# Scan resets, PSUM bank order and two moved steps in the attention units of an RWKV and two-MLP kernel

## The chip, the cores and the metric

The kernel runs on one core of one Trainium2 chip. The metric is the device time of one execution in microseconds; the time of a kernel is the median of several executions. PE is TensorE (matrix products and transposes), DVE is VectorE, ACT is ScalarE, POOL is GpSimd, and SP issues most of the DMAs.

## What is computed

Three stages follow each other: a linear attention with a decaying state (4 batches, 8 heads, 768 positions, head size 48), an expert layer in which each of the 3072 tokens goes to one of 8 experts, and a dense layer with a squared ReLU. In float32, from the reference:

```python
for t in range(S):
    kt, vt, rt, wt = (k[:, :, t], v[:, :, t], r[:, :, t], w[:, :, t])
    cur = np.einsum('bhd,bhe->bhde', u[None] * kt, vt)
    y[:, :, t] = np.einsum('bhd,bhde->bhe', rt, state + cur)
    state = wt[:, :, :, None] * state + np.einsum('bhd,bhe->bhde', kt, vt)
...
logits = x @ w_gate;  e_idx = np.argmax(logits, axis=1)
out[mask] = gate_w[mask, None] * eom[mask, e, None] * (np.maximum(x[mask] @ w1[e], 0.0) @ w2[e])
...
h = x @ w_in;  r = np.maximum(h, 0.0);  return (r * r) @ w_out
```

## The kernel before

**Units.** The attention is cut into 16 units (`NU`), each one batch and two heads, so four units make a batch. A unit's 768 positions are six chunks of 128 (`NC`), each in two halves of 64 (`HT`). For each half, running products of the decay w are needed forwards from the half's start (`ff`, in `prefix`) and backwards from its end (`suf`, in `suffix`). One scan instruction on DVE makes these products for all six chunks at once: the six stretches of 64 lie in a row of 390 with a zero ahead of each stretch, and at that place the scan adds a start value out of the vector `f_1`, so that the running product begins anew there. `suffix` runs two scans: the one of the second half (q = 1) starts from ones (`s_1`); the one of the first half (q = 0) starts from the results of the former, which L688 copies into `f_1`. `prefix` runs two: the first starts from reciprocals (L697), the second from the results of the first, which L699 copies into `f_1`. Both kinds of reset write the same 128x391 vector in turn.

**One iteration of the loop (L843 to L885).** The order of the work on PE, DVE, ACT, SP and POOL is written out by hand: each engine takes its instructions in the order of the calls. Iteration t does, in this order, for the units t - 1, t, t + 1 and t + 2: the loads; `gate_products` of t + 1 (POOL, two products into the one buffer `g1`); `scores` of the first three chunks of t (PE, copied by ACT, masked on POOL by a select, L743); `k_back` of t (PE transposes, copied by ACT into `kP`); `prefix` of t + 1 (DVE); `within` of t - 1 (PE); `states` of t (PE); `state_scan` of t (DVE, L755); `scores` of the last three chunks; `spread` of t + 1 (ACT); `across` of t - 1 (PE, copied by ACT); `k_turn` and `r_turn` of t + 1 (PE transposes, multiplied on DVE by `suf` into `kT`, L708, and by `ff` into `rA`, L713); `w_turn` of t + 2 (PE); `bonus_in` of t (PE, needs the gate values `gv`); `gate_sum` (DVE, L723) and `gate_values` (POOL, L726) of t + 1; `suffix` of t + 2 (DVE); `back` of t - 1 (PE). At t = 0 `gate_sum` and `gate_values` of unit 0 itself come after `prefix` of unit 1.

**Routing.** As soon as a batch has its output, its tokens are routed in small steps that are dealt out over the next units by place and iteration (`PLAN`, `LAST`, places "back", "scan", "turned", "gate"): products with the gate weights on PE, some twenty small operations on DVE, and six indirect scatters into `x_rows` on POOL. For the last batch but one this ends in iteration 15 at the place "scan". `rows_A` (L256, on DVE) works out which token rows the first expert block, block A, gathers; it stands in iteration 15 at the place "back", ahead of `state_scan` of unit 15. In the same iteration eight splits of weights of block A follow on DVE ("turned", L341), the gathers of the rows on POOL ("gate", L402) and, in iteration 16, their scaling on DVE (L413). `finish_routing` sorts the experts by count; L289 there compares with a table `ek` of expert numbers that one iota of POOL makes at the start (L132).

**PSUM banks.** The class `Ring` (L643) hands out four banks in turn to whoever asks: two to the first scores, two to `k_back`, one to `states`, two to the last scores, two each to `k_turn`, `r_turn` and `back`, and one now and then to routing. So which earlier user a step has to wait for depends on the order of the asking. In `k_turn` of t + 1 the first bank is one of `k_back`, the second is that of `states`, which is free when `state_scan` has read it.

**After the units** come block A, one block with few rows, the expert blocks 1 to 7 and the dense layer, all bound together by data: the routing of the last batch is queued on PE behind the transposes of block A's rows.

Of the kernel before, what the change touches and what calls it, by code (L numbers as in the profile page):

```python
# [9 lines left out]
F32 = mybir.dt.float32  # L10
# [4 lines left out]
ALU = mybir.AluOpType  # L15
AX = mybir.AxisListType
# [5 lines left out]
def rwkv_moe_kernel(  # L22
# [15 lines left out]
    nc = tc.nc  # L38
    B, H, S, D = r.shape
    NT, DM = out.shape  # L40
    E, _, F = w1.shape
# [77 lines left out]
    def routing_constants():  # L119
        nonlocal e8, ei, ek, keyc, slot, tile0, over  # L120
        nc.gpsimd.memset(ones, 1.0)
# [9 lines left out]
        ei = iota("ei", [128, E], [[1, E]])  # L131
        ek = iota("ek", [128, E, E], [[1, E], [0, E]])  # L132
        keyc = cst.tile([128, E], F32, name="keyc")
# [12 lines left out]

    e8 = ei = ek = keyc = slot = tile0 = over = None

# [132 lines left out]
    def finish_routing():  # L281
# [6 lines left out]
        nc.vector.tensor_reduce(key, be, axis=AX.X, op=ALU.add)  # L288
        nc.vector.tensor_tensor(be, row(key), ek, op=ALU.is_equal)  # L289
        yield  # L290
# [287 lines left out]
    with ExitStack() as actx:  # L578
# [11 lines left out]
        u_bc = ac.tile([128, H, D], F32, name="u_bc")  # L590
        f_1 = ac.tile([128, NL + 1], F32, name="f1")
        s_1 = ac.tile([128, NL + 1], F32, name="s1")
# [4 lines left out]
        warm = bia[0:1, 2:3]  # L597
        none = f_1[:, 1:L]
        zw = [ps_u.tile([128, NL + 1], F32, name="zw") for _ in range(2)]
# [53 lines left out]
        class Unit:  # L653
# [29 lines left out]
            def suffix(self, z=zw):  # L683

                self.suf = wk.tile([128, 2, NL + 1], F32, name="suf")
                for q in (1, 0):
                    if q == 0:
                        nc.vector.tensor_copy(f_1[:, L::L], self.suf[:, 1, 1::L])  # L688
                    nc.vector.tensor_tensor_scan(out=self.suf[:, q, ::-1], data0=z[q][:, ::-1], data1=(s_1 if q else f_1)[:, ::-1],  # L689
                                                 initial=0.0, op0=ALU.mult, op1=ALU.add)  # L690

            def prefix(self, z=zw):

                self.ff = wk.tile([128, 2, NL], F32, name="ff")
                for q in range(2):
                    if q == 0:
                        nc.vector.reciprocal(f_1[:, 0:NL:L], self.suf[:, 0, 1::L])  # L697
                    else:
                        nc.vector.tensor_copy(f_1[:, 0:NL:L], self.ff[:, 0, HT::L])  # L699
                    nc.vector.tensor_tensor_scan(out=self.ff[:, q], data0=z[q][:, :NL], data1=f_1[:, :NL], initial=0.0, op0=ALU.mult, op1=ALU.add)  # L700

# [27 lines left out]
            def k_back(self):  # L729
                self.kP = wk.tile([128, NC, 2, 64], F32, name="kP", bufs=1)  # L730
                for q, pt in enumerate(self.turn(self.kT)):
                    nc.scalar.copy(self.kP[:, :, q], pt)

            def scores(self, hf):
                A = self.A[hf] = wk.tile([128, HC, 2, C], F32, name=f"A{hf}")
                pa = [ring.tile([128, HC, C], F32, name="pt") for j in range(2)]
                for ci in range(HC):
# [53 lines left out]
        def at(i, st, *a):  # L791
            if 0 <= i < NU:
                getattr(units[i], st)(*a)
# [21 lines left out]
        def first_block_step(t, place):  # L815
# [6 lines left out]
            if NU - 2 <= t < NU and place == "back":  # L822
                for f in range(2 * (t - NU + 2), 2 * (t - NU + 2) + 2):
                    first["A"].prep_w(f, nc.vector, part="hi")
            if (t, place) == (NU - 1, "back"):
                rows_A(rw)
# [16 lines left out]
        for t in range(-1, NU + 1):  # L843
# [6 lines left out]
            first_block_step(t, "loads")  # L850
            if t + 1 < NU - 1:
                at(t + 1, "gate_products")
# [6 lines left out]
            if t == 0:  # L859
                at(t, "gate_sum")  # L860
                at(t, "gate_values")
            at(t - 1, "within")
            at(t, "states")
            at(t, "state_scan")
            at(t, "scores", 1)
            at(t + 1, "spread")
            at(t - 1, "across")
            step(t, "scan")
            at(t + 1, "k_turn")
            at(t + 1, "r_turn")  # L870
# [525 lines left out]
```

## Time and profile before

| | |
|---|---|
| time, median of 3 runs | 844.82 us (844.03 to 846.26) |
| profiled execution, its own time | 843.21 us |
| its span, first to last instruction | 841.4 us, 15700 instructions, mean granted clock 0.991 |
| busy in the span | PE 801.0 us (95%), DVE 543.2 (65%), ACT 374.1 (44%), POOL 351.9 (42%) |
| chain that ended last, by engine | PE 62%, DVE 15%, issue 14%, POOL 4%, DMA 2% |
| costliest lines of DVE in that chain | L689 3%, L700 2%, L713 2%, L708 1%, L755 1% |

The page also cuts the span into 40 slices of 21 us. Each digit is the busy share in tenths (9 is 90% or more):

```profile
PE   5999999878999999999999999999999999999995
DVE  7799999956567777887633878888633434434342
ACT  4566665632544545455544344343433333333321
POOL 7665868535335445544653334243311212223121
PEclk9999999989999999999999999999999999999998
DMA  9576777414659577678751233232204113032011
```

The attention units fill the first eight slices. A share of busy time is an average over what runs in a slice; which engine ends a wait there is read from the timelines. The ends of PE's products are modelled, so PE at 90% is not PE at its peak.

### The profile page before, as it was taken

To read this page: it belongs to the slowest core of one execution; us is meant where nothing else is said; L and a number is where in the kernel's file an instruction comes from. 1 tells how busy PE (TensorE), PEld (TensorE's weight loads), DVE (VectorE), ACT (ScalarE), POOL (GpSimd) and SP (SyncE) were. 2 spreads that over 40 slices of the span, in tenths; PEclk is the share of its full clock that TensorE was granted. 3 is DMA by queue.
4 is the path that set the end of the run, shared out by engine and by line. 5 is a ranking of instruction groups with operands and counts; after the bars stand their busy time and mean duration, and the time that the engine had idled before them with its cause. 6 is when DMAs were issued, how large, how long until landed. Compare 5 with 4: busy or idle time off the path is not lost.

```text
span 841.4 us, 15700 instructions
## 1 busy us (share of the span) xinstructions
PE 801.0 (95%) x5964; PEld 725.0 (86%) x5964; DVE 543.2 (65%) x977; ACT 374.1 (44%) x792; POOL 351.9 (42%) x433
## 2 busy tenths in 40 slices
PE   5999999878999999999999999999999999999995
PEld 4888787758889999999999998888899999999994
DVE  7799999956567777887633878888633434434342
ACT  4566665632544545455544344343433333333321
POOL 7665868535335445544653334243311212223121
PEclk9999999989999999999999999999999999999998
DMA  9576777414659577678751233232204113032011
GB/s 180 117 144 118 159 149 187 164 53 156 207 105 258 137 252 191 188 195 277 142 180 48 93 114 94 76 102 85 76 1 141 45 69 112 11 104 76 1 47 38
DMA packets 157365, 102.90 MB, mean 122 GB/s; under 512 B 112350, under 2 KB 140942, under 8 KB 157286
## 3 DMA queue, kind: packets, MB, share of 16 engines
q1 hardware_dynamic: 149046, 86.55, 38.8%
q0 software_dynamic: 4912, 14.65, 5.3%
q8 instruction: 48, 0.79, 0.4%
q10 hardware_dynamic: 3328, 0.66, 0.4%
q14 instruction: 31, 0.25, 0.1%
HBM read 79.34 MB, written 22.50 MB: 121 GB/s over the span
## 4 chain that ended last, share of the span: by engine, by line
PE 62%; DVE 15%; issue 14%; POOL 4%; DMA 2%; ACT 0%; POOLq 0%; DVEq 0%; SPq 0%; ACTq 0%
PE ph L346 9%; PE ph L347 9%; PE ph L348 9%; PE po L346 5%; PE po L348 5%; PE px L348 5%; PE po L347 5%; PE px L346 5%; PE px L347 5%; DVE suf L689 3%; POOL out_dram L1185 2%; DVE ff L700 2%; DVE rA L713 2%; DVE kT L708 1%; DVE St L755 1%
## 5 line engine op out<-in xcount | busy, mean ns | idle before, releaser
L1160 DVE SCALAR_TENSOR_TENSOR gg<-ph,rl 128x512 f32<-128x512 f32 x96 | 66.2, 689 | 121.8 <-ACT rl L1158 111.3
L1158 ACT ACTIVATE rl<-ph 128x512 f32<-128x512 f32 x96 | 57.4, 598 | 145.8 <-PE ph L348 137.0
L341 DVE TENSOR_TENSOR gl<-gg,gh 128x512 fp32r<-128x512 f32 x96 | 66.7, 695 | 65.9 <-ACT gh L339 41.9
L339 ACT CAST gh<-gg 128x512 fp32r<-128x512 f32 x96 | 59.6, 621 | 103.5 <-DVE gg L1160 103.5
L341 POOL TENSOR_TENSOR w1l<-w1r,w1h 128x384 fp32r<-128x384 f32 x56 | 59.5, 1069 | 66.9 <-ACT w1h L339 66.5
L335 ACT ACTIVATE hh<-ph 128x320 fp32r<-128x320 f32 (+7 forms) x64 | 32.4, 507 | 112.1 <-PE ph L348 99.1
L1106 POOL TENSOR_TENSOR caf<-caf,cbf 128x384 f32<-128x384 f32 x32 | 32.5, 1017 | 114.0 <-DVE cbf L1105 114.0
L341 DVE TENSOR_TENSOR w2l<-w2r,w2h 128x384 fp32r<-128x384 f32 x64 | 63.6, 997 | 20.1 <-ACT w2h L339 19.0
L336 DVE SCALAR_TENSOR_TENSOR hl<-ph,hh 128x320 fp32r<-128x320 f32 (+7 forms) x64 | 36.8, 576 | 36.5 <-ACT hh L335 30.8
L1185 POOL DMA_INDIRECT out_dram<-ob,tokc x24 | 23.4, 975 | 67.2 <-DVE ob L1183 65.0
L346 PE MATMUL po<-hh,w2h 128*128 128x320 f32 (+4 forms) x120 | 42.3, 352 | 0.0
L347 PE MATMUL po<-hl,w2h 128*128 128x320 f32 (+4 forms) x120 | 41.3, 345 | 0.0
L348 PE MATMUL po<-hh,w2l 128*128 128x320 f32 (+4 forms) x120 | 41.2, 344 | 0.0
L341 POOL TENSOR_TENSOR x22l<-x2r,x22h 128x512 fp32r<-128x512 f32 x12 | 15.5, 1293 | 51.5 <-ACT x22h L339 51.5
L740 PE MATMUL pt<-rA,kT 64*128 64x128 f32 x300 | 31.7, 301 | 4.4 <-DVE rA L713 4.4
L341 POOL TENSOR_TENSOR x21l<-x2r,x21h 128x512 fp32r<-128x512 f32 x12 | 15.6, 1296 | 45.5 <-ACT x21h L339 45.5
L402 POOL DMA_INDIRECT xg<-x_rows,gi x28 | 29.0, 1034 | 11.0 <-issue 4.9
L339 ACT CAST w2h<-w2r 128x384 fp32r<-128x384 f32 x64 | 32.9, 516 | 0.0
L247 POOL DMA_INDIRECT x_rows<-xr,dsi x24 | 24.3, 1011 | 20.7 <-DVE vals L240 14.3
L339 ACT CAST w1h<-w1r 128x384 fp32r<-128x384 f32 x64 | 32.7, 512 | 0.0
L743 POOL TENSOR_SCALAR_AFFINE_SELECT A<-A 128x768 f32<-128x768 f32 x32 | 27.7, 873 | 10.4 <-ACT A L742 10.4
L726 POOL TENSOR_TENSOR gv<-vN,g 128x576 f32<-128x576 f32 x16 | 18.4, 1153 | 32.1 <-issue 14.2
(863 smaller groups left out, 2655.1 us busy)
## 6 DMA issues: line engine op xcount, KB each, us to landing
w1r<-in_moe_w_dram SPq DMA_DIRECT2D x16, 768.0 KB
w2r<-in_moe_w_dram SPq DMA_DIRECT2D x16, 768.0 KB
x2r<-x_cols SPq DMA_DIRECT2D x12, 768.0 KB
cq<-in_moe_w_in_dram SPq DMA_DIRECT2D x16, 384.0 KB
cq<-in_moe_w_out_dram SPq DMA_DIRECT2D x16, 384.0 KB
vN<-in_v_dram SPq DMA_DIRECT2D x32, 144.0 KB
part<-ob SPq DMA_DIRECT2D x24, 192.0 KB
ob<-part SPq DMA_DIRECT2D x24, 192.0 KB
```

The lines of the kernel that those rows point to most:

```text
L335: nc.scalar.activation(hi, src, AF.Relu)
L336: nc.vector.scalar_tensor_tensor(lo, src, 0.0, hi.bitcast(F32), op0=ALU.max, op1=ALU.subtract)
L339: nc.scalar.copy(hi, src)
L341: lo_eng.tensor_tensor(lo, src, hi.bitcast(F32), op=ALU.subtract)
L346: nc.tensor.matmul(out_, a_of(ah), b_of(bh), start=start, stop=False)
L347: nc.tensor.matmul(out_, a_of(ah), b_of(bl), start=False, stop=False)
L348: nc.tensor.matmul(out_, a_of(al), b_of(bh), start=False, stop=stop)
L740: nc.tensor.matmul(pa[j][:, ci], self.kT[pp, hf * HC + ci], self.rA[pp, hf * HC + ci], start=True, stop=True)
L1106: nc.gpsimd.tensor_tensor(af, af, bf, op=ALU.add)
L1158: nc.scalar.activation(rl, ph, AF.Relu)
L1160: nc.vector.scalar_tensor_tensor(gg, ph, 0.0, rl, op0=ALU.max, op1=ALU.mult)
L1185: ins = nc.gpsimd.indirect_dma_start(out=out[:, :], out_offset=IndirectOffsetOnAxis(ap=tokc[:, n:n + 1], axis=0), in_=ob, in_offset=None)
```

## The change

- `f_1` gets a second row. The first keeps the resets of the suffix scan and of the first prefix scan, the second holds those of the second prefix scan.
- In `suffix` the copy of the six reset values becomes a reduce with a maximum over one element each.
- In `prefix` one reciprocal of 12 elements, from both halves of `suf`, takes the place of a reciprocal of 6 and a copy of 6. Both scans of `prefix` now start from values that are known before either of them.
- `score_banks` asks for the two banks of the last scores right after `within`, ahead of `states`; the scores themselves stay where they were.
- `rows_A` moves from "back" to a new place "scan" of iteration 15, behind `state_scan`, the last scores, `across` and the last scatter step.
- `gate_products` of unit 1 moves from the start of iteration 0 to behind `gate_values` of unit 0.
- The table `ek` is gone; the comparison reads the vector `ei`, broadcast.

```diff
-        ek = iota("ek", [128, E, E], [[1, E], [0, E]])
...
-        nc.vector.tensor_tensor(be, row(key), ek, op=ALU.is_equal)
+        nc.vector.tensor_tensor(be, row(key), col(ei), op=ALU.is_equal)
...
-        f_1 = ac.tile([128, NL + 1], F32, name="f1")
+        f_1 = ac.tile([128, 2, NL + 1], F32, name="f1")
...
                 for q in (1, 0):
                     if q == 0:
-                        nc.vector.tensor_copy(f_1[:, L::L], self.suf[:, 1, 1::L])
-                    nc.vector.tensor_tensor_scan(out=self.suf[:, q, ::-1], data0=z[q][:, ::-1], data1=(s_1 if q else f_1)[:, ::-1],
+                        nc.vector.tensor_reduce(f_1[:, 0, L::L], self.suf[:, 1, 1::L].rearrange("p (c o) -> p c o", o=1), axis=AX.X, op=ALU.max)
+                    nc.vector.tensor_tensor_scan(out=self.suf[:, q, ::-1], data0=z[q][:, ::-1], data1=(s_1 if q else f_1[:, 0])[:, ::-1],
                                                  initial=0.0, op0=ALU.mult, op1=ALU.add)
...
+                nc.vector.reciprocal(f_1[:, :, 0:NL:L], self.suf[:, :, 1::L])
                 for q in range(2):
-                    if q == 0:
-                        nc.vector.reciprocal(f_1[:, 0:NL:L], self.suf[:, 0, 1::L])
-                    else:
-                        nc.vector.tensor_copy(f_1[:, 0:NL:L], self.ff[:, 0, HT::L])
-                    nc.vector.tensor_tensor_scan(out=self.ff[:, q], data0=z[q][:, :NL], data1=f_1[:, :NL], initial=0.0, op0=ALU.mult, op1=ALU.add)
+                    nc.vector.tensor_tensor_scan(out=self.ff[:, q], data0=z[q][:, :NL], data1=f_1[:, q, :NL], initial=0.0, op0=ALU.mult, op1=ALU.add)
...
+            def score_banks(self):
+                self.pa = [ring.tile([128, HC, C], F32, name="pt") for j in range(2)]
+                return self.pa
+
             def scores(self, hf):
...
-                pa = [ring.tile([128, HC, C], F32, name="pt") for j in range(2)]
+                pa = self.pa if hf else self.score_banks()
...
-            if (t, place) == (NU - 1, "back"):
+            if (t, place) == (NU - 1, "scan"):
                 rows_A(rw)
...
-            if t + 1 < NU - 1:
+            if t and t + 1 < NU - 1:
                 at(t + 1, "gate_products")
...
             if t == 0:
                 at(t, "gate_sum")
                 at(t, "gate_values")
+                at(t + 1, "gate_products")
             at(t - 1, "within")
+            at(t, "score_banks")
             at(t, "states")
...
             step(t, "scan")
+            first_block_step(t, "scan")
```

## Rows read from the trace of the kernel before

**Rows 1.** Busy by stretches: us, PE, PEld, DVE, ACT, POOL, granted clock, DMA share, GB/s:

```profile
84.00:105.00 21.00, 19.49 (x347) 16.65 (x345) 19.80 (x35) 12.81 (x31) 17.46 (x23) 1.00 0.72 160
...
294.00:841.00 547.00, 537.01 (x2758) 493.35 (x2756) 309.56 (x485) 218.93 (x425) 185.56 (x193) 1.00 0.35 106
```

**Rows 2.** Groups by line, 0 to 260 us (count, busy us, mean ns, idle before):

```profile
L688 DVE COPY f<-suf 128x6 f32<-128x6 f32 x16 | 10.9, 680 | 0.6
...
L699 DVE COPY f<-ff 128x6 f32<-128x6 f32 x16 | 6.8, 423 | 0.5
```

**Rows 3.** DVE timeline, one unit: start, us, operation, [idle before <- releaser]:

```profile
34.35 0.41 DVE L688 COPY f<-suf 128x6 f32<-128x6 f32 x1
...
36.02 0.97 DVE L700 TENSOR_TENSOR_SCAN ff<-zw,f 128x390 f32<-128x390 f32 x1
...
37.67 0.97 DVE L700 TENSOR_TENSOR_SCAN ff<-zw,f 128x390 f32<-128x390 f32 x1
38.56 0.73 DVE L755 TENSOR_TENSOR_SCAN St<-pt,P 128x288 f32<-128x288 f32 x1
39.91 0.56 DVE L708 TENSOR_TENSOR kT<-pa,suf 128x384 f32<-128x384 f32 x1 [0.62 <-PE pa L668]
...
43.43 0.41 DVE L688 COPY f<-suf 128x6 f32<-128x6 f32 x1
```

**Rows 4.** DVE timeline, two small operations at 100 to 108 us:

```profile
100.90 2.40 DVE L688 COPY f<-suf 128x6 f32<-128x6 f32 x1
...
107.31 0.22 DVE L186 TENSOR_REDUCE mx<-lg 128x6 f32<-128x48 f32 x1
```

**Rows 5.** POOL timeline, what ran beside those two:

```profile
101.84 1.42 POOL L718 TENSOR_TENSOR g<-kN,rN 128x576 f32<-128x576 f32 x1
...
107.25 0.86 POOL L743 TENSOR_SCALAR_AFFINE_SELECT A<-A 128x768 f32<-128x768 f32 x1 [0.38 <-ACT A L742]
```

**Rows 6.** PE timeline, where a step begins in one unit:

```profile
90.44 0.94 PE L740 MATMUL pt<-rA,kT 64*128 64x128 f32 x12 [0.35 <-DVE rA L713]
...
96.05 0.27 PE L668 MATMUL pt<-ident,kN 64*128 64x64 f32 x1
...
118.02 0.62 PE L668 MATMUL pt<-ident,kN 64*128 64x64 f32 x12
...
120.11 0.86 PE L668 MATMUL pt<-ident,xT 64*128 64x64 f32 x12
```

**Rows 7.** DVE timeline, the first kT product of units 5 and 6:

```profile
58.08 1.02 DVE L708 TENSOR_TENSOR kT<-pt,suf 128x384 f32<-128x384 f32 x2 [0.62 <-PE pt L668]
...
69.08 1.00 DVE L708 TENSOR_TENSOR kT<-pt,suf 128x384 f32<-128x384 f32 x2
```

**Rows 8.** DVE timeline, the first kT product of units 9 and 10:

```profile
97.38 1.02 DVE L708 TENSOR_TENSOR kT<-pt,suf 128x384 f32<-128x384 f32 x2 [0.62 <-PE pt L668]
...
109.56 0.53 DVE L708 TENSOR_TENSOR kT<-pa,suf 128x384 f32<-128x384 f32 x1
```

**Rows 9.** POOL timeline, the first gate product of unit 1:

```profile
17.31 1.42 POOL L718 TENSOR_TENSOR g<-kN,rN 128x576 f32<-128x576 f32 x1 [4.21 <-DVE g L723]
```

**Rows 10.** PE timeline, before and at the bonus of unit 0:

```profile
19.42 0.95 PE L676 MATMUL zw<-ident,wN 64*128 64x64 f32 x12
22.24 0.87 PE L764 MATMUL py<-ident,gv 128*128 128x128 f32 x6 [1.87 <-POOL gv L726]
```

**Rows 11.** Busy time by stretches, 24 to 28 us (columns as in rows 1):

```profile
24.00:26.00 2.00, 2.00 (x27) 1.88 (x25) 1.86 (x5) 1.88 (x5) 1.92 (x3) 0.50 1.13 224
26.00:28.00 2.00, 2.00 (x38) 1.95 (x37) 0.54 (x1) 1.28 (x3) 1.81 (x2) 0.71 0.59 120
```

**Rows 12.** DVE timeline, the end of the units:

```profile
165.62 0.14 DVE L257 TENSOR_SCALAR mA<-cum 128x1 f32<-128x1 f32 x1
...
169.28 0.76 DVE L755 TENSOR_TENSOR_SCAN St<-pt,P 128x288 f32<-128x288 f32 x1 [0.55 <-PE py L781]
...
178.84 0.53 DVE L413 TENSOR_SCALAR xg<-xg 128x384 f32<-128x384 f32 x1 [4.10 <-DMA xg<-x_rows,gA]
```

More of the change, by code (lines that the diff above doesn't have):

```diff
@@ L119, in routing_constants @@
     def routing_constants():
-        nonlocal e8, ei, ek, keyc, slot, tile0, over
+        nonlocal e8, ei, keyc, slot, tile0, over
         nc.gpsimd.memset(ones, 1.0)
@@ L145, in routing_constants @@
         reset_routing()
-    e8 = ei = ek = keyc = slot = tile0 = over = None
+    e8 = ei = keyc = slot = tile0 = over = None
     def reset_routing():
@@ L597, in rwkv_moe_kernel @@
         warm = bia[0:1, 2:3]
-        none = f_1[:, 1:L]
+        none = f_1[:, 0, 1:L]
         zw = [ps_u.tile([128, NL + 1], F32, name="zw") for _ in range(2)]
```

## The prediction

> **What bounds the kernel now.** I read the 40 slices of the page first: PE is nearly full from the second slice to the last, DVE is busy for most of the first fifth of the span and at a third of it later. The table of busy time by stretches says the same in numbers [rows 1]: from 294 us on PE works 537.01 of 547 us at a granted clock of 1.00, so nothing but PE sets the pace there; from 84 to 105 us, inside the attention units, DVE works 19.80 of 21 us and PE 19.49. The change touches only the units (0 to some 170 us). What it takes from them should therefore come off the end one for one, since every later stage starts from data of the one before. The chain of waits, read in order of time, runs through DVE in most units: scan, reset copy, scan, reciprocal, scan, reset copy, scan, state scan, then a short wait for PE, then the products. So the second view is DVE's timeline of one unit without routing [rows 3]: the same copy comes at 34.35 and 43.43, one unit is 9.08 us. The third question is how far behind DVE the next engine is, and that is PE [rows 6].
>
> **Reset copies.** The two groups take 10.9 and 6.8 us for 16 copies each of 128x6 [rows 2], in the mean 680 and 423 ns. One such copy lasts 2.40 us, from 100.90 to 103.30 [rows 4]; beside it POOL runs a product from 101.84 to 103.26 [rows 5], and the copy ends as that ends: it is held by POOL's work. The reduce at 107.31 takes 0.22 us [rows 4] although POOL's select runs from 107.25 to 108.11 [rows 5]. A maximum over one element is such a reduce, with 6 inputs in place of 48, so I price it at 0.19, between 0 and 0.22. The first copy thus gives back 10.9 - 16 x 0.19 = 7.9 us of DVE. The second copy goes altogether, and with it the dependence between the two prefix scans: from one to the next it is 1.65 us now (36.02 to 37.67), while a scan with no dependence behind it lets the next operation start after 0.89 (37.67 to 38.56) [rows 3]. That is 0.76 us in a clean unit. The merged reciprocal writes 12 elements for 6; no row shows that size beside this one, so its growth is bounded by 0 and by one more small operation, 0.22 [rows 4]; I take 0.04, since the reduce over 48 elements needs no more than 0.22 in all.
>
> The Trainium skill (VectorE: DVE Perf Modes, Rules for kernel authors) speaks against this part: a reduce on the hot path is called the slowest operation of this engine, to be expected at single rate. At six elements the row of 0.22 us with 48 inputs does not bear that out as a cost; by the page the rate would matter only for long rows.
>
> **Score and state banks.** Four PSUM banks are handed out in turn. Before, the states' bank came ahead of the two score banks, so the second bank of the next unit's k transposes was the states' bank and had to wait for the state scan: DVE then sits 0.62 us before kT, released by PE [rows 3, 7, 8]. After, that bank is one that ScalarE has copied out long before the state scan, and the states' bank goes to the last r transposes, which DVE needs 0.9 us (two kT products [rows 8]) later. I cost the new order at nothing otherwise; what hides it is across, which PE runs in between. If ScalarE were late, the wait would return, 0.62 at most.
>
> **Clean unit.** DVE: 9.08 - 0.22 (copy to reduce, 0.41 to 0.19) - 0.76 - 0.62 + 0.04 = 7.5 us [rows 3]. PE: from the scores to the next k transposes 5.61 (90.44 to 96.05), from there over r and w transposes and the bonus to the back transposes 2.09 (118.02 to 120.11), the twelve back transposes between 0.4 and the 0.62 of the same twelve [rows 6]: 8.1 to 8.3, and between 0 and 0.35 waiting for rA [rows 6]. I take 8.27. So PE becomes the bound, the unit goes from 9.08 to 8.27, and 0.81 of the 1.56 that DVE gives up reaches the end. Three units run so (2 to 4): 2.4 us. Ends: 0.4 (9.08 - 8.3 - 0.35) and 1.56 each, 1.2 to 4.7.
>
> **Routed units.** Ten units (5 to 14) also carry routing on PE and DVE. In three of them PE has 24 routing products more. One takes 11.00 us with no long copy (58.08 to 69.08 [rows 7]), and there PE, not DVE, is the last to arrive at the state scan: no gain. The other two take 12.2 each (one of them 97.38 to 109.56 [rows 8]) because of the 2.40 us copy; they fall to 11.00, 1.18 each. The remaining seven I put at the clean unit's 0.81: 5.7. Sum 8.0. Ends: the two long copies alone, 2.4, and the full 1.1 of DVE work per unit, 11.
>
> **First gate products.** At the first step POOL starts unit 1's gate product only at 17.31, held 4.21 us for DVE's sum of unit 0 [rows 9], and A's select and unit 0's gate values queue behind its two halves. PE is done with the w transposes at 20.37 and stands until 22.24 for those values [rows 10]. After, the values of unit 0 go first and the products second, and the bonus can start when PE gets there: 22.24 - 20.37 = 1.9 us, and 0.3 for the copies of unit 0, which lie on the same path (an estimate, under the 0.76 of a clean unit): 2.2. Behind the moved products stands the select of unit 0's second scores. Counted from 17.31 it is done at the latest after values no longer than a product, two products and itself: 17.31 + 1.42 + 2.84 + 0.86 = 22.4 [rows 5, 9]; PE wants it after the bonus and the scores, 20.07 + 0.87 + 0.94 = 21.9 at the earliest [rows 6, 10]. So up to 0.5 may be lost to this wait. After PE stood still the granted clock is 0.50, the 1.2 GHz level, from 24 to 26 us, and 0.71 from 26 to 28 [rows 11]; at half pace that costs 1.0 + 0.6 = 1.6 us. If the shorter stand leaves the clock up, this comes back too. Ends 1.7 and 3.8; I take 3.0. The Trainium skill (TensorE: Matmul & The Clock Gate, Part 1) says an idle PE falls to the lower clock; the row agrees, and by that rule the sum would use 3.8.
>
> **First rows.** Their index work runs from 165.62 to 168.73 ahead of the state scan of unit 15, which then waits another 0.55 for PE [rows 12]. Moved behind it, the state scan can only come earlier, but across of unit 15 is not what the gathers wait for; they wait for scatters in POOL's queue. So gain 0. Queued behind the moved work are eight splits of weights, which shift by up to 3.1 us; DVE now stands 4.10 us before 178.84 [rows 12], so 1.0 of cover is left. Without that cover the gathered rows would be scaled late by what exceeds it. One index table less on POOL at the start lies beside the first loads: 0.
>
> **Sum.** 3.0 + 2.4 + 8.0 = 13.4 us against the profiled execution, 843.2 - 13.4 = 829.8; its span is 841.4 and some 1.8 lie around it. The median of the runs shown is 1.6 above that execution, so the forecast against the median 844.8 is 831.4; I say 832, for small waits that pass to ScalarE.
>
> **Rivals.** (1) PE holds the units harder than I summed: every unit costs PE its 8.3 and the whole 0.35 for rA, and in routed units ScalarE's copies add as much again. Then only the start (2.2), the two long copies (2.4) and 0.4 in each clean unit remain, 5.8 us: 839. For it: PE is at 19.49 of 21 now [rows 1]. Against: part of that busy time is PE waiting for the banks. (2) DVE's whole saving comes out, because PE's busy time is partly stretched waiting: the upper ends, 3.8 + 4.7 + 11 = 19.5: 825. Against: the 8.1 of PE are starts in sequence without idle. (3) The reduce is held by POOL as the copy was: then the two long stalls stay, 11 us are left, 834, still within the forecast. (4) Nothing measurable: the units end earlier but the gathers at the end wait for something else. Against: scatters and gathers follow the last unit's gate sums through one queue. 844. (5) Slower, by the clock: tighter units could make PE alternate work and short stands so that the granted clock stays at 0.50 as at 24 us [rows 11]. Each us at half clock loses half a us, so with 13 gained it decides beyond 26 us of such stretches in the units; 32 of them give 844.8 - 13.4 + 16 = 847. Against: PE gets busier, and in the units it stood at 1.00 [rows 1].
>
> **How the numbers follow.** Forecast (827 to 836) 0.72; rival 1 (836 to 842) 0.14; rival 2 below 827 0.05; rival 4 0.06; rival 5 0.03. Rival 3 is inside the forecast. The range 827 to 839 leaves out rival 2's part, the upper part of rival 1 (0.05), 4 and 5: 0.19. 0.3% is 2.5 us, about what a measurement of this kernel can tell from no change: faster 0.91, same 0.06, slower 0.03.
>
> **What would show it.** In the trace after: the reduce at 0.15 to 0.22 us in all 16 units with none near 2; prefix scans 0.9 apart; no wait of DVE before kT released by PE right after the state scan, but one of PE's own making, in clean units of 8.2 to 8.4 us; the bonus of unit 0 near 20 us; the scaling of the first rows still released by the DMA and not by splits. The prediction is wrong if clean units stay near 9 us, if PE's sequence has gaps of its own, or if the end of the units moves and the first products of the experts do not.

## The result and the profile after

The changed kernel takes 833.27 us (median of 4 runs, 832.23 to 835.88) beside 845.54 us for the kernel before, measured with it: a ratio of 0.986, 95% interval 0.982 to 0.989, 12.3 us less. The forecast was 832.0 with a range of 827 to 839. The profiled execution took 832.55 us with a span of 830.7 us (before 843.21 and 841.4), and DVE is busy for 531.0 us instead of 543.2.

The first view is DVE's timeline of a unit without routing in the changed kernel (start, us, operation, in brackets the idle time before it and what ended it). It answers [rows 3].

```profile
34.73 0.56 DVE L704 TENSOR_TENSOR kT<-pa,suf 128x384 f32<-128x384 f32 x1 [0.82 <-PE pt L667]
...
38.26 0.17 DVE L687 TENSOR_REDUCE f<-suf 128x6 f32<-128x6 f32 x1
...
39.47 0.23 DVE L694 RECIPROCAL f<-suf 128x12 f32<-128x12 f32 x1
39.73 1.83 DVE L696 TENSOR_TENSOR_SCAN ff<-zw,f 128x390 f32<-128x390 f32 x2
...
43.03 1.02 DVE L704 TENSOR_TENSOR kT<-pt,suf 128x384 f32<-128x384 f32 x2 [0.82 <-PE pt L667]
```

The reduce stands at 0.17 us where the copy took 0.41, the two prefix scans take 1.83 us together, and a unit is 8.30 us (34.73 to 43.03). The wait before kT has not gone. It has grown from 0.62 to 0.82 us: it is now what DVE has left over until PE gets there.

The same in busy time by stretches (us, PE, PEld, DVE, ACT, POOL, granted clock, DMA share, GB/s); the first two rows answer [rows 11], the last is the stretch that answers [rows 1], moved by the 8 us that the units are earlier there:

```profile
24.00:26.00 2.00, 2.00 (x36) 1.76 (x35) 1.86 (x3) 1.82 (x6) 2.00 (x3) 1.00 0.92 180
26.00:28.00 2.00, 2.00 (x46) 1.76 (x45) 1.56 (x4) 0.72 (x2) 0.75 (x1) 1.00 0.29 55
...
76.00:97.00 21.00, 20.21 (x372) 17.26 (x366) 18.57 (x36) 13.69 (x33) 17.70 (x23) 1.00 0.85 184
```

PE and DVE have changed places: PE 20.21 of 21 us (19.49 before), DVE 18.57 (19.80). The half clock at 24 to 28 us is gone.

The best ruler in this case is the start of a unit's first kT, since every unit has one and since two kernels can be laid side by side by it. The table gives it against the kernel before, for the units 2, 5 and 15, then what lies between unit 2 and unit 15, and the times (median, and that of the kernel before on the same chip).

| kernel | unit 2 | unit 5 | unit 15 | units 2 to 15 | us | before |
|---|---|---|---|---|---|---|
| changed kernel | -4.39 | -6.74 | -11.61 | -7.22 | 833.27 | 845.54 |
| resets alone | -2.67 | -5.03 | -9.84 | -7.17 | 835.38 | 844.95 |
| bank order alone | -0.06 | -0.81 | -1.19 | -1.13 | 843.95 | 844.95 |
| first gate products alone | -2.26 | -2.31 | -2.23 | +0.03 | 842.72 | 844.95 |
| first rows alone | -0.02 | -0.04 | -0.03 | -0.01 | 844.25 | 844.95 |
| changed, copy back | -3.46 | -5.70 | -7.64 | -4.18 | 837.57 | 845.19 |
| changed, products left out | -3.62 | -5.98 | -11.60 | -7.98 | 833.95 | 845.19 |
| changed, early routing step | -3.50 | -5.85 | -11.68 | -8.18 | 832.98 | 845.19 |
| changed, products by token | -3.88 | -6.24 | +4.39 | +8.27 | 849.53 | 845.19 |
| changed, held operations | -3.95 | -6.30 | -9.87 | -5.92 | 834.85 | 844.54 |
| bank order, waits by tile | +0.83 | +0.11 | -0.48 | -1.31 | 842.21 | 844.54 |
| changed, tail clock | -4.45 | -6.80 | -11.58 | -7.13 | 831.56 | 844.54 |
| changed, both | -3.82 | -6.17 | -11.94 | -8.12 | 831.39 | 844.46 |

For the first five kernels, what unit 15 gains and what the median gains agree within 1 us (11.6 and 12.3; 9.8 and 9.6; 1.2 and 1.0; 2.2 and 2.2; 0 and 0.7). So by the medians the end of the units passes on to the end of the kernel one for one, as forecast, to within 1 us. The spans of the profiled executions show 0.7 to 1.7 us less (10.7 for 11.6 us at unit 15, 8.9 for 9.8, -0.5 for 1.2, 0.5 for 2.2, -0.7 for 0.0): the profiled execution of the kernel before lies 1.6 us below its median. Unit 2 itself moves by up to 1 us between executions with the same work ahead of it (last section), so effects inside the units are read from unit 2 on.

### The profile page after: what moved, and what is told of

It is laid out like the page before. It is cut to its first block, busy times and chain, and to the rows that moved or that the text cites. A ratio compares the mean times of both kernels' runs of the same rounds, so it can differ in the third digit from the quotient of the medians.

```text
span 830.7 us, 15691 instructions
## 1 busy us (share of the span) xinstructions
PE 799.4 (96%) x5964; PEld 724.5 (87%) x5964; DVE 531.0 (64%) x961; ACT 374.3 (45%) x792; POOL 352.3 (42%) x432
## 4 chain that ended last, share of the span: by engine, by line
PE 59%; issue 12%; POOL 4%; DVE 0%; POOLq 0%; ACT 0%; DVEq 0%; ACTq 0%
PE ph L345 10%; PE ph L346 10%; PE ph L347 10%; PE po L345 5%; PE po L347 5%; PE po L346 5%; PE px L347 5%; PE px L345 5%; PE px L346 5%; POOL out_dram L1188 2%; PE px L431 1%; PE po L431 0%; POOL x21l L340 0%; POOL x22l L340 0%; POOL x20l L340 0%
## 5 line engine op out<-in xcount | busy, mean ns | idle before, releaser
L401 POOL DMA_INDIRECT xg<-x_rows,gi x28 | 29.0, 1036 | 10.7 <-issue 5.2
L340 POOL TENSOR_TENSOR x20l<-x2r,x20h 128x512 fp32r<-128x512 f32 x12 | 15.5, 1295 | 35.9 <-ACT x20h L338 35.9
```

What stands on the lines that cost most here:

```text
L340: lo_eng.tensor_tensor(lo, src, hi.bitcast(F32), op=ALU.subtract)
```

## The experiments

**The four parts by themselves** (the resets with the smaller index table that makes room for their second row). Theory A is that of the prediction: POOL's work holds the reset copies, and PE is the bound behind DVE. The rivals say of each part that it only uncovers another wait. First the resets:

```diff
-nc.vector.tensor_copy(f_1[:, L::L], self.suf[:, 1, 1::L])
+nc.vector.tensor_reduce(f_1[:, 0, L::L], self.suf[:, 1, 1::L]..., axis=AX.X, op=ALU.max)
...
+nc.vector.reciprocal(f_1[:, :, 0:NL:L], self.suf[:, :, 1::L])
```

> The kernel before with the resets alone: the reduce for the first copy, one reciprocal for both prefix scans, and the smaller index table that makes room for them. Theory A (POOL holds the copies, PE is the next bound at 8.3 us a unit): the reduce lasts 0.17 us in all units, a clean unit goes from 9.08 to 8.3 to 8.5, the wait for PE before kT stays, since the states' bank still stands in the way of the k transposes; first kT of unit 15 6 to 7.5 us earlier, 837 to 839.5. Rival B (the copies only filled time in which DVE would have waited for PE): the wait before kT grows by what the copies gave, units stay near 9 us, 843 to 845.

Measured: 835.38 us, ratio 0.988 (0.985 to 0.991), a little better than A had it (837 to 839.5). DVE's timeline of this kernel, two units:

```profile
36.45 0.56 DVE L704 TENSOR_TENSOR kT<-pa,suf 128x384 f32<-128x384 f32 x1 [0.83 <-PE pt L667]
...
44.75 0.56 DVE L704 TENSOR_TENSOR kT<-pt,suf 128x384 f32<-128x384 f32 x1 [0.83 <-PE pt L667]
```

A unit takes 8.30 us with the old order of the banks too, with the same wait, and PE's timeline shows no idle time at the k transposes in these two units. From unit 2 to unit 15 the resets alone give 7.17 of the 7.22 us. Rival B falls, and so does a part of A: the order of the banks is not needed for 8.3 us.

The order of the banks:

```diff
+            at(t, "score_banks")
             at(t, "states")
```

> The kernel before with the order of the banks alone. Theory A: the 0.62 us that DVE waits before kT is the states' bank, it goes in clean units, which take 8.5 us, and mostly in the others; unit 15's first kT is 4 to 6 us earlier, 839.5 to 841.5. Rival C (the k transposes come late because PE has across before them, whatever the bank): the wait stays, nothing moves by more than 0.1 us a unit, 845.

Measured: 843.95 us, ratio 0.999 (0.997 to 1.000). Unit 15 is 1.19 us earlier, neither the 4 to 6 of A nor the nothing of C. DVE's timeline of units 3, 4 and 5, then PE's row at unit 3:

```profile
39.84 0.56 DVE L708 TENSOR_TENSOR kT<-pa,suf 128x384 f32<-128x384 f32 x1 [0.62 <-PE pt L668]
...
47.57 0.73 DVE L759 TENSOR_TENSOR_SCAN St<-pa,P 128x288 f32<-128x288 f32 x1
48.22 1.00 DVE L708 TENSOR_TENSOR kT<-pt,suf 128x384 f32<-128x384 f32 x2
...
55.92 0.73 DVE L759 TENSOR_TENSOR_SCAN St<-pt,P 128x288 f32<-128x288 f32 x1
57.27 1.02 DVE L708 TENSOR_TENSOR kT<-pt,suf 128x384 f32<-128x384 f32 x2 [0.62 <-PE pt L668]
```

```profile
39.28 0.27 PE L668 MATMUL pt<-ident,kN 64*128 64x64 f32 x1 [0.56 <-DVE St L759]
```

The wait goes in unit 4 and stays in units 3 and 5. Ahead of unit 4's kT the state scan reads the fourth bank (`St<-pa` in its row), ahead of those of units 3 (at 38.49 us) and 5 one of the pool of three (`St<-pt`). Where it stays, PE's transposes still wait for the state scan, although by the order of asking their bank should be another.

The first gate products:

```diff
-            if t + 1 < NU - 1:
+            if t and t + 1 < NU - 1:
                 at(t + 1, "gate_products")
...
                 at(t, "gate_values")
+                at(t + 1, "gate_products")
```

> The kernel before with unit 1's gate products behind the values of unit 0 alone. Theory A (the start is worth 4 us, half of it the clock): unit 0's bonus near 19.5 to 20.4, granted clock 1.00 from 24 to 28 us, unit 2's first kT 3 to 4 us earlier and all later ones by the same, 841 to 842.5. Rival D (most of the 4.4 us at unit 2 came from the resets, which also lie there): 1 to 2 us, 843.5 to 844.5.

Measured: 842.72 us, ratio 0.996 (0.995 to 0.997). A's picture, in size between A and D: unit 0's bonus begins at 19.73 instead of 22.24, the granted clock stays up, and every unit from 2 on is 2.2 to 2.3 us earlier. PE's row and a stretch:

```profile
19.73 0.87 PE L764 MATMUL py<-ident,gv 128*128 128x128 f32 x6
```

```profile
26.00:28.00 2.00, 0.62 (x11) 0.36 (x7) 1.90 (x3) 1.25 (x3) 1.90 (x3) 1.00 0.34 64
```

PE works for only 0.62 of the 2 us from 26 on: with the old resets DVE works on there (1.90 us) and PE has to wait, so not all of the returned clock is used. The resets alone also keep the clock up at 24 to 28 us (1.00), with the bonus at 21.15. Together the two give 4.39 us at unit 2, by themselves 2.26 and 2.67, each to within the 1 us by which unit 2 moves between executions.

The first rows:

```diff
-            if (t, place) == (NU - 1, "back"):
+            if (t, place) == (NU - 1, "scan"):
                 rows_A(rw)
```

> The kernel before with the first rows' index work behind the state scan alone. Theory A (off the path: 1 us of cover is left before the first scaling): first scaling of gathered rows within 0.3 us of before, 845 within 1 us; the state scan of unit 15 still waits for PE. Rival E (the half clock after the units is stretched by it): the stretch at half clock ahead of the first scaling grows from 7 toward 13 us and the time rises by 1 to 2 us, 846 to 847.

Measured: 844.25 us, ratio 0.998 (0.9970 to 0.9998), unit 15 0.03 us earlier, the first scaling of gathered rows at 179.36 instead of 178.84 us. The stretch at half clock did get longer, as E had it (182 to 193 us instead of 181 to 188), but the time did not rise. The interval just leaves out no change, by 0.2 us, and no row shows what would have moved; I take it as no effect.

**Is the copy held by POOL's work?**

```diff
-nc.vector.tensor_reduce(f_1[:, 0, L::L], self.suf[:, 1, 1::L]..., axis=AX.X, op=ALU.max)
+nc.vector.tensor_copy(f_1[:, 0, L::L], self.suf[:, 1, 1::L])
```

> The changed kernel with the suffix reset as the old copy (the merged reciprocal stays). Theory A (POOL's work holds the copy, the reduce is not held): the copies last 0.4 to 2.4 us, those beside a product of POOL longest; clean units stay at 8.3, since 0.8 us of DVE's wait for PE covers a copy of 0.41, and only the long copies show: first kT of unit 15 2 to 5 us later, 835 to 838. Rival B (the copy is no slower than the reduce once it is alone between the scans): 0.2 us each, unit 15 within 0.5 us, 833.

Measured: 837.57 us, ratio 0.991 (0.987 to 0.994); unit 15 is 3.97 us later than in the changed kernel, 3.04 of it after unit 2. A holds. Clean units have copies of 0.41 us and still take 8.3; the two copies beside the products of POOL are longer than forecast (2.92 us for the other one), and the shortest of the 16 takes 0.17 us, no more than the reduce. So the copy is not slow in itself.

```profile
93.86 3.10 DVE L687 COPY f<-suf 128x6 f32<-128x6 f32 x1
```

Beside it POOL has the end of a scatter (to 94.33 us), the gate values (94.37 to 95.53) and the next product (95.51 to 96.92), and the copy ends at 96.96: it was held until more than one operation of POOL in a row had ended. From unit 2 to unit 15 this kernel, which keeps the merged reciprocal, is still 4.18 us shorter than the kernel before. So the reduce accounts for 3.04 of the 7.22 us. That the rest comes from the merged reciprocal, by the second copy and the dependence between the prefix scans, is what is left; no run has that part alone.

What I had not foreseen stands in the groups of DVE by line up to 170 us (count, busy us, mean ns, idle before), here of this kernel and then of the changed one:

```profile
L687 DVE COPY f<-suf 128x6 f32<-128x6 f32 x16 | 11.9, 742 | 0.6
L224 DVE TENSOR_TENSOR_SCAN ex<-ones,inc 128x8 f32<-128x8 f32 x3 | 1.8, 590 | 0.0
L220 DVE TENSOR_TENSOR tail<-sg 128x6 f32<-128x6 f32 x3 | 1.6, 521 | 0.1
L187 DVE TENSOR_TENSOR z<-lg,mx 128x48 f32<-128x48 f32 x3 | 1.3, 431 | 0.1
L233 DVE CAST dsi<-dst 128x6 int32<-128x6 f32 x3 | 1.2, 408 | 0.2
L199 DVE TENSOR_TENSOR zo<-lg,oh 128x48 f32<-128x48 f32 x3 | 1.2, 397 | 0.1
L221 DVE COPY xr<-tail 128x12 f32<-128x12 f32 x3 | 0.5, 174 | 0.1
L225 DVE TENSOR_TENSOR bof<-ex,inc 128x8 f32<-128x8 f32 x3 | 0.5, 172 | 0.1
L217 DVE TENSOR_SCALAR sg<-sg 128x6 f32<-128x6 f32 x3 | 0.5, 172 | 0.1
```

```profile
L687 DVE TENSOR_REDUCE f<-suf 128x6 f32<-128x6 f32 x16 | 2.7, 166 | 0.6
L199 DVE TENSOR_TENSOR zo<-lg,oh 128x48 f32<-128x48 f32 x3 | 2.5, 822 | 0.1
L225 DVE TENSOR_TENSOR bof<-ex,inc 128x8 f32<-128x8 f32 x3 | 1.8, 584 | 0.1
L221 DVE COPY xr<-tail 128x12 f32<-128x12 f32 x3 | 1.7, 556 | 0.1
L217 DVE TENSOR_SCALAR sg<-sg 128x6 f32<-128x6 f32 x3 | 1.2, 405 | 0.1
```

The reduce takes 9.2 us less than the copies (11.9 to 2.7). Four small routing operations take 4.5 us more (2.7 to 7.2), but four others that are long with the copies take 3.4 us less (ex, tail, z and dsi, 5.8 to 2.5, or 0.5 to 0.8 each in the changed kernel): what is held beside POOL's work changes from one small operation to another. All 72 routing operations of DVE in the units together take 16.7 us in the kernel before, 18.4 with the copy back and 19.4 in the changed one. So 1.0 of the 9.2 us came back as longer routing; against the kernel before it is 2.8 us, of the 14.4 that the two copies took beyond what replaced them.

**Which work of POOL holds them now?**

```diff
+                if 1 < self.un < NU - 1:
+                    self.g1 = units[1].g1
+                    return
                 eng = nc.vector if self.un == NU - 1 else nc.gpsimd
```

> The changed kernel, with POOL's two gate products left out for units 2 to 14, which use those of unit 1. Theory A (the hold moved from the reset copies to routing's small operations, 0.75 to 0.87 us each): those fall to 0.15 to 0.25 us, units with routing get shorter by about 0.5 us each where one was held, first kT of unit 15 2 to 3.5 us earlier, 829.5 to 831.5. Rival F (PE sets the routed units, the held operations lie beside its work): they get shorter just so, but unit 15 moves by less than 0.7 us, 832.5 to 833.5.

Units 2 to 14 go on with the products of unit 1; their own are left out.

Measured: 833.95 us, ratio 0.987 (0.984 to 0.991). Unit 15 stands where it stood, 0.76 us less from unit 2 on. A's expectation is wrong: three of the four groups stay as long as they were. The condition of F, that they get shorter, is not met either, so this run does not decide between the two. DVE's row and POOL's beside it:

```profile
71.39 0.76 DVE L221 COPY xr<-tail 128x12 f32<-128x12 f32 x1
```

```profile
71.25 0.87 POOL L746 TENSOR_SCALAR_AFFINE_SELECT A<-A 128x768 f32<-128x768 f32 x1 [3.37 <-ACT A L745]
```

The copy lasts until the select ends (72.15 and 72.12). In the changed kernel the same pair stands at 70.64 and 70.50, and every routing operation of 0.75 us or more in the units runs beside a select of the scores and ends with it. So it is the select, not the gate products, that holds them. Of the four groups only zo got shorter without the products (822 to 397 ns in the mean), in the second and third unit with 24 products, which are 0.25 us shorter each.

**What bounds the units with 24 routing products?** The changed kernel takes 10.95, 11.49 and 11.54 us for them. PE's rows of the second of them, then DVE's:

```profile
90.37 1.93 PE L170 MATMUL pt<-xT,wcat 128*32 128x256 f32 x24
94.64 0.39 PE L178 MATMUL pa<-ident,lt 96*128 96x96 f32 x2
```

```profile
97.28 0.76 DVE L755 TENSOR_TENSOR_SCAN St<-pt,P 128x288 f32<-128x288 f32 x1 [1.54 <-PE pt L750]
...
100.41 0.53 DVE L704 TENSOR_TENSOR kT<-pa,suf 128x384 f32<-128x384 f32 x1
```

DVE waits 1.54 us for PE's states, and then has 2.5 us of routing ahead of kT. So one routing step went ahead of the state scan, and ScalarE's copy of the logits ahead of its check of w:

```diff
-PLAN = (..., (5, "scan"), (5, "scan"), ...
+PLAN = (..., (5, "pre"), (5, "scan"), ...
...
+            step(t, "pre")
             at(t, "state_scan")
```

> The changed kernel with the first of two routing steps that follow the state scan in the units with 24 routing products put ahead of it, where DVE waits 1.05 to 1.56 us for PE, and ScalarE's copy of the logits ahead of its check of w. Theory A (in these three units PE's own sequence, 11.0 us, is the bound just behind DVE): the step's 1.25 us leave the path but PE gives back only 0.4 to 0.6 us in two of the units and 0.1 in the first, unit 15 about 1 us earlier, 832 to 833. Rival G (the chain from PE's last state product over the state scan and the routing steps to kT is the bound, PE follows): 1.2 us in each of the three, unit 15 3.7 us earlier, 829.5.

Measured: 832.98 us, ratio 0.985 (0.982 to 0.989); 0.96 us less from unit 2 to 15: 0.43, 0.24 and 0.29 in the three units. A's number, but with the units the other way round (it had 0.1 in the first and 0.4 to 0.6 in the others), and its reason holds only in the first, where DVE ends up waiting for PE. In the other two the moved operations (0.21 us each in the changed kernel) were held again, first by a product of POOL (until 97.50 in the unit shown), then by a select (until 98.31), and the state scan came later for it. DVE's rows:

```profile
96.60 0.96 DVE L187 TENSOR_TENSOR z<-lg,mx 128x48 f32<-128x48 f32 x1
97.59 0.79 DVE L191 SCALAR_TENSOR_TENSOR cand<-z,e 128x48 f32<-128x48 f32 x1
...
98.81 0.75 DVE L755 TENSOR_TENSOR_SCAN St<-pt,P 128x288 f32<-128x288 f32 x1
```

The other attempt was to give PE less work in these units, by turning the products round:

```diff
-nc.tensor.matmul(pl[32 * g:32 * g + 32, :GW], wcat[:, pr], xT[:, pr, g * GW:(g + 1) * GW], ...)
+nc.tensor.matmul(pl[:, 32 * i:32 * i + 32], xT[:, pr, 128 * i:128 * i + 128], wcat[:, pr], ...)
```

> The changed kernel with the routing products of the first three batches turned round: tokens as weights and 32 columns moving, so that the logits come out by token and the two transposes and one copy go. PE's 24 products took 1.93 us and the transposes 0.39. Theory A (PE sets these units, directly or through the state scan that waits for it): whatever PE saves in them, 0.4 to 1.5 us each, comes out at the next kT, unit 15 1.2 to 4.5 us earlier in equal parts from three units and none from the others, 829 to 832. Rival H (routing's DVE and ScalarE work sets them): unit 15 moves by less than 0.5 us.

Measured: 849.53 us, ratio 1.005 (1.003 to 1.006). My guess that PE would save was wrong by far, so the run does not test what A and H said. PE's row and a stretch:

```profile
53.19 6.28 PE L170 MATMUL pt<-wcat,xT 128*128 128x32 f32 x48
```

```profile
58.00:60.00 2.00, 2.00 (x19) 1.94 (x21) 0.66 (x1) 0.34 (x1) 0.61 (x1) 0.50 0.80 159
```

In the first unit the products take 6.28 us instead of 1.93 + 0.39, 4.0 more: each of the 48 passes has its own load of 128x128 weights. In the other two it is 5.46 and 6.89. In all three the granted clock falls to 0.50 during or right after them, and PE's work behind is stretched as well (the scores' twelve products of the first from 0.95 to 1.60 us). The three units get 5.90, 4.01 and 5.63 us longer, and the others stay within 0.1 us. With PE this much longer, PE sets these units. That it also sets them at its former length does not follow; there the rows above show DVE waiting 1.54 us for PE and then working without a break up to kT.

**Taking the held operations away.**

```diff
-nc.vector.tensor_copy(xr[:, :, DM:], tail[:, b])
+nc.scalar.copy(xr[:, :, DM:], tail[:, b])
...
-nc.vector.tensor_tensor_scan(out=ex, ..., data1=pkv[:, :, NTB], ...)
-nc.vector.tensor_tensor(bof[:, b], ex, pkv[:, :, NTB], op=ALU.subtract)
+nc.vector.tensor_tensor_scan(out=bof[:, b], ..., data1=inc0[:, :E, NTB], ...)
```

> The changed kernel with the early routing step of the run before, and two of the operations that POOL's select holds taken off DVE: the copy of 128x12 goes to ScalarE, and the subtract behind the scan of counts goes, since the scan runs over counts shifted by one. Theory A (in the units with routing but without the 24 products DVE is the bound, so a held operation costs its whole length): 0.5 to 0.75 us less in four of these units beside the 0.96 us of the early step, from unit 2 to unit 15 2.8 to 3.9 us less than in the changed kernel, 829 to 830.5. Rival I (the select holds the next operation in their place, or PE sets these units too): from unit 2 to 15 0.7 to 1.7 us less, 832 to 833.

The early routing step is in this kernel too. Measured: 834.85 us, ratio 0.990 (0.988 to 0.992). From unit 2 to unit 14 it is 1.34 us less than the changed kernel, 0.96 of which the early step gives: rival I. Each half of I has its row, two of DVE, then one of ScalarE and one of PE:

```profile
71.40 0.56 DVE L709 TENSOR_TENSOR kT<-pt,suf 128x384 f32<-128x384 f32 x1 [0.76 <-PE pt L672]
...
79.06 0.83 DVE L232 TENSOR_TENSOR rk<-inc,bof 128x48 f32<-128x48 f32 x1
```

```profile
143.60 0.20 ACT L223 COPY xr<-tail 128x12 f32<-128x12 f32 x1 [4.09 <-DVE tail L222]
```

```profile
144.29 0.27 PE L672 MATMUL pa<-ident,kT 64*128 64x64 f32 x1 [2.46 <-ACT xr L792]
```

Where the copy of 0.75 us was, DVE now waits 0.76 us for PE: that unit takes 9.1 us either way. Where the subtract was held, the next operation with both inputs in SBUF is held in its place (0.83 us, 0.21 in the changed kernel). And unit 14 is 2.64 us longer: ScalarE's copy waits 4.09 us in its queue for DVE's routing, the copies that empty two banks stand behind it, and PE waits 2.46 us for them. A small operation given to an idle engine brought a wait into that engine's queue.

**Why did the bank order gain so little?**

```diff
-tc.tile_pool(name="ps_t", bufs=3, space=PSUM, side="right")
+tc.tile_pool(name="ps_t", bufs=3, space=PSUM, side="right", reuse_waits="tile")
```

> The kernel before with the order of the banks, and the pool of three of the four banks told to wait for the tile that a bank held last. Theory J (the order alone gained 1.19 us because the k transposes still waited for the state scan wherever the states' bank came from the same pool as theirs, though not for its data): the wait of 0.62 us before kT goes in units 3, 4 and 5, first kT of unit 15 2.8 to 3.8 us earlier than in the kernel before, near 842. Rival K (the transposes are late for a reason of their own): as with the order alone, 1.2 us.

Measured: 842.21 us, ratio 0.998 (0.997 to 0.999). The time is J's number, but not by J's way: from unit 2 to 15 it is 1.31 us less, as with the order alone, unit 15 is only 0.48 us earlier, and the wait of 0.62 us is still there in units 3 and 5. Theory J falls. What is left is that the k transposes get the states' bank itself again. The class `Ring` names the fourth bank in turn, but the other three come from a pool, and the rows of units 3 and 5 show the transposes waiting for the state scan where the states' bank is one of that pool. No trace shows bank numbers, so that the pool does not hand out its three in turn is inferred and not shown. Shown is that, of units 3 to 5, only where the states have the fourth bank, outside the pool (unit 4), does the new order do what it was meant to do.

**The clock behind the units.** In the changed kernel the granted clock is 0.50 from 170 to 182 us, about twice the stretch of before. Eight products whose result is not used keep PE busy while it waits for the first gathered rows:

```diff
+        idle_work(6)
         blkA.prep_x(0)
+        idle_work(2)
         blkA.prep_x(1)
```

> The changed kernel with eight products of 256 columns added on PE while it waits for the first gathered rows, their result unused. Theory A (the stretch at half clock behind the units is hidden by the transfers of the last batch's rows): the stretch from 168 to 182 us gets shorter by at least 5 us, the time stays within 1 us of 833.3. Rival L (work that PE does not get done in this stretch is missing later, so each us at half clock costs half a us): 2 to 5 us less, 828.5 to 831.5. If the products do not hold the clock up they only show their own length: 833 to 834.

Measured: 831.56 us (831.13 to 832.44), ratio 0.985 (0.983 to 0.986). Stretches of the changed kernel (first row) and of this one:

```profile
170.00:172.00 2.00, 1.75 (x7) 0.97 (x7) 0.81 (x4) 0.85 (x2) 0.00 (x0) 0.50 0.04 0
```

```profile
170.00:172.00 2.00, 2.00 (x21) 1.50 (x21) 0.61 (x2) 0.94 (x3) 0.00 (x0) 1.00 0.05 0
...
200.00:202.00 2.00, 2.00 (x6) 1.52 (x6) 2.00 (x8) 0.49 (x2) 0.00 (x0) 0.50 0.00 0
```

The clock is up from 164 to 198 us. The 13 us at half pace that went are worth some 6 us of PE's work (an estimate, half of 13), and the span got 1.4 us shorter. The next rows that PE waits for come by DMA, PE stands there instead (1.83 us before 197.41), and a stretch at half clock follows at 199 to 202 us. The result, 1.7 us less, lies between A (within 1 us) and L (2 to 5).

Both additions together:

> The changed kernel with the early routing step and with the eight added products behind the units. If PE's bound in the units with 24 products and the clock behind the units are separate costs, they add: from unit 2 to unit 15 0.9 to 1.0 us less than in the changed kernel, granted clock 1.00 from 164 to some 195 us, and 833.3 - 1.0 - 1.5 = 830.8, between 829.8 and 832. If the end of the units is not what the experts' first products wait for once the clock is up, only one of the two comes out: 831.5 to 832.5.

Measured: 831.39 us (829.93 to 833.29), ratio 0.985 (0.984 to 0.987). From unit 2 to 15 it is 0.90 us less, as expected of the early step. The clock did not stay up this time (0.50 from 172 to 180 us), and yet span (829.3 us) and time are those of the run before. The time lies in the first range of the expectation, but the granted clock that it was built on did not come, so neither half of the expectation is shown. In these two executions a longer stretch at half clock behind the units (170 to 180 us here, 199 to 202 there) cost at most the 0.4 us by which unit 15 is earlier here, and where the 1.4 us of that run come from stays open. These two kernels are 1.7 and 1.9 us below the median of the changed one; the intervals of their ratios lie inside its own, so it is not shown that they beat it, only that they beat the kernel before.

## Why the prediction came out, step by step

**Reset copies: right.** The reduce lasts 0.17 us in all 16 units (priced 0.19), the merged reciprocal 0.23 (priced 0.19 + 0.04), the scans stand 0.89 apart (0.89). That POOL's work holds a copy and not a reduce is shown by the copy put back. The copy of 2.40 us [rows 4] was held by more than the product that I named: POOL's gate values run ahead of that product, from 100.70 to 101.87 us, and the copy begins beside them. The Trainium skill (SBUF — State Buffer, Who interferes with whom) says the same in general: copies and operations with one scalar in the two-port modes, and operations with both inputs in SBUF, contend with instructions of POOL that read SBUF, a reduce on this chip never does. The runs agree, with 0.17 to 3.10 us for the copy and 0.17 throughout for the reduce, and the subtract, the products of the routing and its copy are of the kinds that the page names.

**Order of the banks: wrong, at no cost.** I took it, as the section on the kernel before has it, that the four banks go round in turn, and that the 0.62 us of DVE before kT would go with the new order. With the new order alone the wait goes only where the states have the fourth bank; that the other three do not go round is the likely reason, not a shown one. In the changed kernel it is PE's own work that ends last there. The resets alone reach 8.30 us a unit. Since I let PE set the clean unit, the error did not reach the sum there.

**Clean units: right.** 8.27 us forecast, 8.30 measured, PE as the bound; three of them gave 2.35 us, forecast 2.4.

**Routed units: the term that was mis-sized.** Unit 5 to unit 15 gave 4.9 us, forecast 8.0. The two units with the long copy gave 0.69 and 0.63 for 1.18 each, the first of the 24-product kind 0.05 for 0, the seven others 3.5 together for 5.7. In the units with the long copy the copy no longer ends last: PE makes the state scan late (1.54 us), and 2.5 us of DVE's routing follow one after the other; with one step of it ahead of the state scan they are 0.24 and 0.29 us shorter. Of the 2.2 us that the seven others lack, 1.8 lie in three of them, units 7, 11 and 14. I had let PE set all seven. In these three DVE's timeline shows no wait, before or after, and routing's operations take 0.70, 0.69 and 0.44 us longer than in the kernel before, as others of them come to stand beside POOL's selects; unit 14 also had short copies to give back (0.41 and 0.17 us). In units 6 and 10 PE is the next bound at 9.1 us, as the run with held operations taken away shows. That run does not show the same for the holds: in units 7 and 11 the next operation was held, and in unit 14 PE came to wait for ScalarE. I had said that the saving of DVE stays saved unless PE comes first, and had not asked which of DVE's other operations would now stand beside POOL's.

**Start: right in mechanism, too small.** Forecast 3.0 with ends of 1.7 and 3.8; unit 2 is 4.39 us earlier in the profiled execution, outside these ends, and 3.5 to 4.5 in the others with the same start. I had put in 0.3 us for the copies; the resets alone give 2.67 us at unit 2, since they too keep the clock up. The bonus of unit 0 came from 22.24 to 19.39 us, 2.85 where I had 2.2, and the half clock at 24 to 28 us [rows 11] went altogether, as the profile of each of the two parts alone shows too. I had put its 1.6 us in at half; whole, the sum would have been 3.8. The A select of unit 0's second scores, which I feared would make PE wait up to 0.5 us, was done at 21.04, in time.

**First rows: right.** Alone it moves unit 15 by 0.03 us; the first scaling is still released by the DMA.

**Sum.** 13.4 us forecast against the profiled execution; measured 11.6 at unit 15 and 10.7 in the span, 12.3 by the medians. Start +1.4, routed units -3.1, and 0.9 us lost behind unit 15: errors of opposite sign. That the forecast of 832 fits better than its parts is partly luck. Of the rivals, (1) has its mechanism right in the 24-product units, (2) is excluded by PE's 8.30, (3) by the reduce's 0.17, (4) by the agreement of unit 15 with the medians, and (5) has its sign turned in the units: the change took stretches at half clock away there, though behind the units the stretch grew from 7 to 13 us.

## What to carry to other kernels

An operation of DVE that is held by POOL's work is worth replacing by a form that is not held, but price it by what comes to stand beside POOL next: here 2.8 of the 14.4 us that DVE was given back went into longer routing operations, 1.8 of them in three units that DVE sets. Add up all the operations, not only those that grew: the holds moved from one small operation to another. Before counting a wait as a gain of its own, ask whether it would be there anyway once the engine behind is the bound; in the changed kernel the bank order and the copy given to ScalarE were both worth nothing for that reason, and the second brought a wait into a queue. Lay the kernels side by side by one instruction that each unit has: it told effects of 0.2 us where the time of a run could not tell 2.

## What the runs showed of the hardware that was not expected

The twelve w transposes of unit 1, at the same place in the same order, take 0.59 us in one execution and 0.95 in another, while the granted clock of these stretches is shown as 1.00 in both. Here the changed kernel and the last one:

```profile
18.86 0.59 PE L675 MATMUL zw<-ident,wN 64*128 64x64 f32 x12
```

```profile
19.11 0.95 PE L675 MATMUL zw<-ident,wN 64*128 64x64 f32 x12
```

Unit 2 begins at 26.43 and 27.00 us accordingly; over the six executions with the same work ahead of it, it lies between 26.37 and 27.32. The Trainium skill (TensorE: Matmul & The Clock Gate, Part 1) says that the number of slow products at a kernel's start varies from run to run. These rows fit that, but no row shows the clock as the cause, since the granted clock does not tell the two apart.

A granted clock of 0.50 also came while PE was busy throughout: in the kernel with products by token PE was busy for all of 54 to 60 us, mostly with products of 32 columns, each with its own load of 128x128 weights, and the clock fell to 0.50 at 58 us.
